# Building decay tables from Sigmoid and reciprocals, with one table load, in a retention and gated-FFN kernel

## The chip, the cores and the metric

The kernel runs on one core of one Trainium2 chip. Its metric is the device time of one execution in microseconds (us). A core has five engines that run their own instruction streams and wait for one another on semaphores: TensorE (PE; its weight loads are shown apart as PEld), VectorE (DVE), ScalarE (ACT), GpSimd (POOL) and SyncE (SP), which here gives out loads and stores. The transfers themselves run on 16 DMA engines. ScalarE computes functions such as Exp or Sigmoid from a table set, and the program holds an ACT_TABLE_LOAD wherever the set changes.

## The reference

Retention with a decay per head, on 8 batches of 8 heads, 576 positions and 64 features, is followed by a gated feed-forward layer on its 4608 x 512 result:

```python
scores = scale * np.matmul(q, k.transpose(0, 1, 3, 2))          # scale = 1/sqrt(64)
gamma = 1.0 - 2.0 ** (-5.0 - np.arange(H))
rel = pos[:, None] - pos[None, :]
Dmat = np.where(rel >= 0, gamma[:, None, None] ** rel[None, :, :], 0.0)
x = np.matmul(scores * Dmat[None], v)                           # then heads are put side by side
gate = 1.0 / (1.0 + np.exp(-(x @ w_gate)))
out = (gate * (x @ w_val)) @ w_out                              # 512 -> 1536 -> 512
```

The decay gamma^(i-j) is split into gamma^i on q and gamma^(-j) on k, so each needs a small table by position and head.

## The kernel before: the parts concerned

The loads of the first four chunks of batch 0 come as pairs (two chunks, four heads at a time). The first k and q are cut in two, one half given out by SyncE, the other by ScalarE:

```python
def load_pair(A):
    b, a2 = PAIRS[A]
    for nm, src, g in (("k", k, 0), ("q", q, 0), ("k", k, 1), ("q", q, 1), ("v", v, 0), ("v", v, 1)):
        t = ld_pool.tile([P, M, 2, D], FP32, tag="ld", ...)
        queues = (nc.sync, nc.scalar) if A == 0 and g == 0 and nm != "v" else (nc.sync,)
        n = M // len(queues)
        for i, queue in enumerate(queues):
            queue.dma_start(out=t[:, i * n:(i + 1) * n]..., in_=src[...]...)
```

TensorE is kept at work from the start with matmuls on a zero tile, of which nothing is used (`fill(10, 4)`: 40 of 128 columns; a plain `fill(n)`: n of 512 columns). Then the tables are made by Exp, first those of the pairs (`qtab2`, `ktab2`), then those of the later chunks (`qtab`, `ktab`); `warm` brings in the Sigmoid set for the gates:

```python
fill(10, 4)
def tables(shape, pattern, step, put, fix=None):
    ...                                          # iota of positions on GpSimd
    for h in range(H):
        nc.vector.tensor_scalar_mul(put(arg, h), pos, math.log(1.0 - 2.0 ** (-5.0 - h)))
    nc.scalar.activation(out=kt, in_=arg, func=AF.Exp, bias=0.0, scale=-1.0)
    nc.scalar.activation(out=qt, in_=arg, func=AF.Exp, bias=lnscale, scale=1.0)
    return qt, kt
qtab2, ktab2 = tables(...)
...
qtab, ktab = tables(...)
nc.scalar.activation(out=warm, in_=lnscale, func=AF.Sigmoid)
for t in sbd:                                    # four 128 x 512 bf16 tiles for states
    nc.vector.memset(t, 0.0)
```

The opening that follows multiplies k (on GpSimd) and q (on VectorE) by the tables (`cast_pair`), turns them on TensorE (`turn`: four transposes into PSUM, then one ScalarE copy to kT or qT), multiplies them (`pair_qk`, result qkp), masks that on VectorE (ptp), and forms the state from k and v (`first_st`, result st):

```python
cast_pair("q", 0, 0, nc.vector)
turn("k", 0, 0, *TR)
turn("q", 0, 0, *PV)
fill(3)
cast_pair("q", 0, 1, nc.vector)
pair_qk(0, 0, QK)
turn("k", 0, 1, *TR)
fill(2)
turn("q", 0, 1, *PV)
...                                              # the same for the second pair
first_st(0, 0)
```

The rest (`h` is a matmul with a gate or value weight, `op` one with the output weight) is a long run of matmuls that the change doesn't touch.

Of the kernel before, what the change touches and what calls it, by code (L numbers as in the profile page):

```python
# [9 lines left out]
FP32 = mybir.dt.float32  # L10
BF16 = mybir.dt.bfloat16
AF = mybir.ActivationFunctionType
ALU = mybir.AluOpType
# [3 lines left out]
def kernel(  # L17
# [19 lines left out]
    nc = tc.nc  # L37

    B, H, S, D = q.shape
    NT, DM = out.shape  # L40
    DFF = moe_w_gate.shape[1]
    P = 128
    M = H // 2
    NC = (S + P - 1) // P
# [3 lines left out]
    consts = ctx.enter_context(tc.tile_pool(name="consts", bufs=1))  # L48
# [18 lines left out]
    LAST = NC - 1  # L67
# [38 lines left out]
    def half(x):  # L106
        return slice(x * 64, x * 64 + 64)
# [17 lines left out]
    def load_pair(A):  # L125

        b, a2 = PAIRS[A]
        for nm, src, g in (("k", k, 0), ("q", q, 0), ("k", k, 1), ("q", q, 1), ("v", v, 0), ("v", v, 1)):
            t = ld_pool.tile([P, M, 2, D], FP32, tag="ld", name=f"{nm}32p_{A}_{g}")
            queues = (nc.sync, nc.scalar) if A == 0 and g == 0 and nm != "v" else (nc.sync,)  # L130
            n = M // len(queues)
            for i, queue in enumerate(queues):
                queue.dma_start(
                    out=t[:, i * n:(i + 1) * n].rearrange("p h r d -> p h (r d)"),
                    in_=src[b, g * M + i * n:g * M + (i + 1) * n,
                            a2 * 2 * P:(a2 + 1) * 2 * P, :].rearrange("h (p r) d -> p h (r d)", r=2))
            parts[nm, "pair", A, g] = t
            yield

# [10 lines left out]
    def load_wo(f):  # L150
        t = ld_pool.tile([P, DM], FP32, tag="ld", name=f"wo32_{f}")
        nc.sync.dma_start(out=t, in_=moe_w_out[f * P:(f + 1) * P, :])
        parts["o", f] = t

    both = [load_pair(A) for A in range(2)]
    for n_pair in (4, 2):
        for one in both:
# [5 lines left out]
    load_w(4, 4)  # L163
    load_w(8, 4)
    pair_2 = load_pair(2)
    for n_wo, n_pair in ((2, 4), (6, 2), (4, 0)):
        for _ in range(n_wo):
# [16 lines left out]
    def fill(n, parts=1):  # L184

        for i in range(n * parts):
            k = 4 // parts
            nc.tensor.matmul(idle[-1][:, 0:k, :], lhsT=blank, rhs=blank.unsqueeze(1).to_broadcast([P, k, P]),  # L188
                             start=True, stop=True)

    fill(10, 4)
    def tables(shape, pattern, step, put, fix=None):

        pos = consts.tile([P, pattern[0][1], pattern[1][1]], FP32, name=f"pos{step}")
        nc.gpsimd.iota(pos, pattern=pattern, base=0, channel_multiplier=step,
                       allow_small_or_imprecise_dtypes=True)
        if fix:
            fix(pos)
        arg = consts.tile(shape, FP32, name=f"arg{step}")
        qt = consts.tile(shape, FP32, name=f"qtab{step}")  # L200
        kt = consts.tile(shape, FP32, name=f"ktab{step}")
        for h in range(H):
            nc.vector.tensor_scalar_mul(put(arg, h), pos, math.log(1.0 - 2.0 ** (-5.0 - h)))
        nc.scalar.activation(out=kt, in_=arg, func=AF.Exp, bias=0.0, scale=-1.0)
        nc.scalar.activation(out=qt, in_=arg, func=AF.Exp, bias=lnscale, scale=1.0)
        return qt, kt

    lnscale = consts.tile([P, 1], FP32)
    nc.vector.memset(lnscale, math.log(1.0 / math.sqrt(D)))
    qtab2, ktab2 = tables([P, 2, H, 2], [[2 * P, 2], [1, 2]], 2, lambda t, h: t[:, :, h, :])  # L210
    ident = consts.tile([P, P], BF16)
    make_identity(nc, ident)


    def last_chunks(pos):
        nc.vector.tensor_scalar_add(pos[half(1), LAST], pos[half(1), LAST], -64.0)

    qtab, ktab = tables([P, NC, H, 1], [[P, NC], [1, 1]], 1, lambda t, h: t[:, :, h, :], last_chunks)
    qtab = qtab.rearrange("p c h o -> p c (h o)")
    ktab = ktab.rearrange("p c h o -> p c (h o)")  # L220
    warm = consts.tile([P, 1], FP32)
    nc.scalar.activation(out=warm, in_=lnscale, func=AF.Sigmoid)


    sbd = [consts.tile([P, M, P], BF16, name=f"sbd{i}") for i in range(4)]
    for t in sbd:
        nc.vector.memset(t, 0.0)

    trip = consts.tile([P, 2, P], BF16)
# [1 line left out]
    for p0 in (0, 64):  # L231
        nc.gpsimd.affine_select(out=trip[p0:p0 + 64], in_=trip[p0:p0 + 64], compare_op=ALU.is_ge, fill=0.0,
                                base=0, pattern=[[-1, 2], [1, P]], channel_multiplier=-2)
# [30 lines left out]
    def cast_pair(nm, A, g, eng):  # L264

        if (nm, A) not in natural:
            natural[nm, A] = osb_pool.tile([P, 2, H, D], BF16, tag="osb", name=f"{nm}p_{A}")
        if nm != "v" and A == 2:
            o = natural[nm, A].rearrange("p r (m y) d -> p y m r d", y=2)[:, g]
        else:  # L270
            o = natural[nm, A][:, :, g * M:(g + 1) * M, :].rearrange("p r h d -> p h r d")
        i = parts.pop((nm, "pair", A, g))
        if nm == "v":
            eng(out=o, in_=i)
        else:
            tab = (ktab2 if nm == "k" else qtab2)[:, PAIRS[A][1], g * M:(g + 1) * M, :].unsqueeze(3).to_broadcast([P, M, 2, D])
            eng.tensor_tensor(out=o, in0=i, in1=tab, op=ALU.mult)
# [51 lines left out]
    def pair_qk(A, g, banks):  # L329
        ps = [psum.tile([P, 2, 2, P], FP32, tag=tag, name=f"qkp_{A}_{g}_{hh}") for hh, (psum, tag) in enumerate(banks)]  # L330
        for i in range(2):
            m = 2 * g + i
            for r in range(2):
                for a in range(2):
                    for hh in range(2):
                        nc.tensor.matmul(ps[hh][half(a), i, r, :], lhsT=turned["kp", A][half(hh), m, r, half(a)],  # L336
                                         rhs=turned["qp", A][half(hh), m, a * P:(a + 1) * P], start=True, stop=True)
        if g == 0:
            probs["p", A] = [att_pool.tile([P, M, 2, P], BF16, tag="T", name=f"ptp_{A}_{hh}", bufs=6) for hh in range(2)]
        for hh in range(2):  # L340
            nc.vector.tensor_tensor(out=probs["p", A][hh][:, 2 * g:2 * g + 2], in0=ps[hh],  # L341
                                    in1=trip.unsqueeze(1).to_broadcast([P, 2, 2, P]), op=ALU.mult)
# [481 lines left out]
    def turn(nm, A, g, pool=ffn_psum, tag="ffn"):  # L824
        pair_t(nm, A, g, pool, tag, on_act)
# [36 lines left out]
    turn("k", 0, 0, *TR)  # L862
    turn("q", 0, 0, *PV)
    fill(3)
    cast_pair("q", 0, 1, nc.vector)
    pair_qk(0, 0, QK)
    turn("k", 0, 1, *TR)
# [233 lines left out]
```

## Time and profile before

| | |
|---|---|
| time, median of 3 | 328.39 us (328.38 to 328.81) |
| span of the profiled execution | 326.8 us |
| VectorE, ScalarE, GpSimd busy | 147.9, 140.7, 104.1 us |
| read from and written to memory | 37.75 and 9.44 MB |
| ACT_TABLE_LOADs | 2, of 1.28 us each, both in the first 6 us |

A busy time is the sum of an engine's instructions; a high share says which engine to look at, while a stage with its own limit has to be read from the timeline. In a row of the timeline the start and the duration come first, in us from the start of the span, then engine, line, operation, tiles with shapes, and in brackets the idle time of the engine ahead of it with what ended it. The chain of work that ended last follows the program back from its end, at each step to what released it; rows of it hold start, duration and what ran. A row of waits gives who waited for whom: total us, times, longest.

### The profile page before, as it was taken

What the parts mean: (1) busy time and instruction counts of PE and PEld (TensorE: products, weight loads), DVE (VectorE), ACT (ScalarE), POOL (GpSimd) and SP (SyncE); (2) the same over time, 40 slices, a digit from 0 to 9 for tenths busy, and PEclk for the clock granted to TensorE, in tenths of its full rate; (3) what the DMA queues carried; (4) which work ended last, traced back from release to release, by engine and by line L of the source; (5) the groups of instructions that cost most, each with busy time, mean ns of one, the idle gap of its engine ahead of it and who ended that gap; (6) DMA issues with size and microseconds to landing.
All of it is one profiled execution on the core that took longest, in us unless ns stands there. A gap on an engine that the chain in (4) does not pass through costs nothing.

```text
span 326.8 us, 8722 instructions
## 1 busy us (share of the span) xinstructions
PE 317.4 (97%) x3584; PEld 170.5 (52%) x3618; DVE 147.9 (45%) x335; ACT 140.7 (43%) x317; POOL 104.1 (32%) x138
## 2 busy tenths in 40 slices
PE   8899999999999999999999999999999999999996
PEld 7664557856546554455445544454445544544443
DVE  6855557656606462355334534344344433404410
ACT  6755545554433353325432553335334533343321
POOL 5774537544364563028200830075003000000000
PEclk9999999999999999999999999999999999999999
DMA  7999999989999999909890899069704810010003
GB/s 218 330 382 376 327 256 243 195 181 168 207 210 192 230 165 239 225 2 221 194 230 0 194 232 224 0 133 225 194 0 121 319 48 0 34 74 27 3 32 96
DMA packets 145849, 55.14 MB, mean 169 GB/s; under 512 B 125200, under 2 KB 137744, under 8 KB 145808
## 3 DMA queue, kind: packets, MB, share of 16 engines
q1 hardware_dynamic: 145120, 54.18, 68.6%
q8 instruction: 28, 0.46, 0.6%
q10 hardware_dynamic: 688, 0.39, 0.4%
q14 instruction: 13, 0.11, 0.1%
HBM read 37.75 MB, written 9.44 MB: 144 GB/s over the span
## 4 chain that ended last, share of the span: by engine, by line
PE 96%; ACT 1%; issue 1%; DVE 1%; ACTq 0%
PE h L731 50%; PE op L798 24%; PE op L980 3%; PE hv L835 3%; PE hg L835 3%; PE val L542 2%; PE idle L188 1%; PE row L516 1%; PE row L524 1%; PE val L558 1%; ACT qT L327 1%; PE op L787 1%; PE hg L906 1%; PE hv L906 1%; PE qkp L336 1%
## 5 line engine op out<-in xcount | busy, mean ns | idle before, releaser
L759 DVE TENSOR_TENSOR gv<-g,h 128x512 bf16<-128x512 bf16 (+1 forms) x96 | 62.8, 654 | 103.2 <-PE h L731 100.5
L731 PE MATMUL h<-xT,wv_sb 128*128 128x512 bf16 (+2 forms) x426 | 100.4, 355 | 0.3
L731 PE MATMUL h<-xT,wg_sb 128*128 128x512 bf16 (+2 forms) x426 | 100.4, 355 | 0.3
L755 ACT ACTIVATE g<-h 128x512 bf16<-128x512 f32 (+1 forms) x96 | 54.7, 570 | 94.3 <-PE h L731 90.2
L798 PE MATMUL op<-wo_sb,gv 128*128 128x512 bf16 x355 | 80.7, 379 | 2.2 <-issue 2.1
L731 PEld LDWEIGHTS <-wg_sb 128*128 128x128 bf16 x432 | 42.0, 98 | 41.2
L731 PEld LDWEIGHTS <-wv_sb 128*128 128x128 bf16 x432 | 42.0, 98 | 40.4
L798 PEld LDWEIGHTS <-gv 128*128 128x128 bf16 x372 | 35.3, 98 | 40.9
L295 POOL CAST v<-v 128x512 bf16<-128x512 f32 x29 | 18.1, 625 | 85.6 <-PE val L542 79.5
L290 POOL TENSOR_TENSOR qk<-k,ktab 128x512 bf16<-128x512 f32 x30 | 31.3, 1042 | 37.0 <-DMA k<-in_k_dram 36.5
L774 ACT COPY ob<-op 128x512 f32<-128x512 f32 x33 | 19.3, 585 | 35.9 <-PE op L798 32.9
L290 POOL TENSOR_TENSOR qk<-q,qtab 128x512 bf16<-128x512 f32 x28 | 29.2, 1042 | 1.9 <-DMA q<-in_q_dram 1.9
L531 DVE TENSOR_TENSOR pt<-row,tri 128x256 bf16<-128x256 f32 x60 | 21.6, 417 | 13.9 <-PE row L524 12.3
L600 ACT CAST xT<-val 128x256 bf16<-128x256 f32 x46 | 15.0, 380 | 22.7 <-PE val L558 18.0
L643 DVE TENSOR_TENSOR s<-s,row 128x256 f32<-128x256 f32 x39 | 16.2, 416 | 1.3
L492 ACT CAST sb<-s 128x256 bf16<-128x256 f32 x44 | 15.9, 420 | 0.3 <-DVE s L643 0.2
L586 DVE COPY glance<-val 128x1 f32<-128x1 f32 x24 | 2.8, 155 | 23.3 <-PE val L558 22.6
L980 PE MATMUL op<-wo_sb,gv 128*128 128x512 bf16 x45 | 11.4, 379 | 0.3 <-issue 0.2
L542 PEld LDWEIGHTS <-v 64*64 64x64 bf16 x480 | 6.2, 108 | 7.5 <-issue 7.2
L558 PE MATMUL val<-T,sb 64*64 64x64 bf16 x368 | 9.7, 195 | 0.3 <-DVE glance L586 0.3
L516 PE MATMUL row<-T 64*64 64x64 bf16 x480 | 9.7, 196 | 0.0
L341 DVE TENSOR_TENSOR ptp<-qkp,trip 128x512 bf16<-128x512 f32 x12 | 7.5, 681 | 3.8 <-PE qkp L336 3.7
(107 smaller groups left out, 236.0 us busy)
## 6 DMA issues: line engine op xcount, KB each, us to landing
out_dram<-ob SPq DMA_DIRECT2D x31, 256.0 KB, 3.1
k<-in_k_dram SPq DMA_DIRECT2D x26, 256.0 KB, 3.9
q<-in_q_dram SPq DMA_DIRECT2D x26, 256.0 KB, 4.1
v<-in_v_dram SPq DMA_DIRECT2D x26, 256.0 KB, 4.5
wg<-in_moe_w_gate_dram SPq DMA_DIRECT2D x12, 256.0 KB, 5.0
wv<-in_moe_w_val_dram SPq DMA_DIRECT2D x12, 256.0 KB, 5.1
wo<-in_moe_w_out_dram SPq DMA_DIRECT2D x12, 256.0 KB, 5.2
v32p<-in_v_dram SPq DMA_DIRECT2D x6, 256.0 KB, 4.9
```

Source lines behind the costliest of these rows:

```text
L290: eng.tensor_tensor(out=natural_qk[s][:, i].rearrange("p m (y d) -> p y m d", y=2), in0=by_halves(loaded[s][1 - i]), in1=tab, op=ALU.mult)
L295: eng(out=natural["v", s], in_=loaded[s][2])
L492: eng(out=state[key], in_=src)
L531: nc.vector.tensor_tensor(out=probs[s][:, y], in0=row_ps[s][y][:, 0], in1=tri.unsqueeze(1).to_broadcast([P, M, 64]), op=ALU.mult)
L643: nc.vector.tensor_tensor(out=new, in0=running[b], in1=p, op=ALU.add)
L731: nc.tensor.matmul(out, lhsT=w_sb[:, kc, fc * P:(fc + 1) * P], rhs=xT[:, kc, t0 + a:t0 + e], start=(kc == 0), stop=(kc == NKC - 1))
L755: nc.scalar.activation(out=g[:, 0:n], in_=h1[:, 0:n], func=AF.Sigmoid)
L759: nc.vector.tensor_tensor(out=gvs[some[0]][:, a:e], in0=g[:, 0:n], in1=h2[:, 0:n], op=ALU.mult)
L774: (eng or on_act)(out=ob, in_=opp)
L798: nc.tensor.matmul(opp, lhsT=gvs[fc][:, nb * P:(nb + 1) * P], rhs=wo_sb[:, fc, :], start=(fc == 0), stop=(fc == NFC - 1))
L835: nc.tensor.matmul(ps, lhsT=(wg_sb if what == "g" else wv_sb)[:, kc, fc * P:(fc + 1) * P], rhs=xT[:, kc, 0:4 * P], start=(kc == 0), stop=( ...
L980: nc.tensor.matmul(opps[nb], lhsT=gvs[fc][:, nb * P:(nb + 1) * P], rhs=wo_sb[:, fc, :], start=(fc == 0), stop=(fc == NFC - 1))
```

## The change

The two exponentials e^a and e^-a are to come from the Sigmoid set, which the gates need anyway: sigmoid(a)/sigmoid(-a) = e^a, and the inverse gives e^-a. ScalarE then needs one table set for the whole kernel, loaded before anything is ready for it, and the set change with `warm` goes. ScalarE also gives out no loads: SyncE gives out the first k and q whole. VectorE gets a Reciprocal and two multiplies for each table in place of the exponentials. The tables of the later chunks, which the opening doesn't use, and two of the four zeroings are finished between the first and the second q multiply.

```diff
-            queues = (nc.sync, nc.scalar) if A == 0 and g == 0 and nm != "v" else (nc.sync,)
-            n = M // len(queues)
-            for i, queue in enumerate(queues):
-                queue.dma_start(...half of the heads...)
+            nc.sync.dma_start(out=t..., in_=src[...all four heads...]...)
 ...
-        nc.scalar.activation(out=kt, in_=arg, func=AF.Exp, bias=0.0, scale=-1.0)
-        nc.scalar.activation(out=qt, in_=arg, func=AF.Exp, bias=lnscale, scale=1.0)
+        def sigmoids(self):
+            nc.scalar.activation(out=self.both[:, 0], in_=self.arg, func=AF.Sigmoid)
+            nc.scalar.activation(out=self.both[:, 1], in_=self.arg, func=AF.Sigmoid, scale=-1.0)
+
+        def powers(self):
+            nc.vector.reciprocal(out=self.inv, in_=self.both)
+            nc.vector.tensor_tensor(out=self.k, in0=self.both[:, 1], in1=self.inv[:, 0], op=ALU.mult)
+            nc.vector.scalar_tensor_tensor(out=self.q, in0=self.both[:, 0], scalar=1.0 / math.sqrt(D),
+                                           in1=self.inv[:, 1], op0=ALU.mult, op1=ALU.mult)
+
+    tabs2 = Tables([P, 2, H, 2], ...)            # the pairs' tables
+    tabs2.args(range(H))
+    tabs2.sigmoids()
 ...
-    warm = consts.tile([P, 1], FP32)
-    nc.scalar.activation(out=warm, in_=lnscale, func=AF.Sigmoid)
+    tabs1 = Tables([P, NC, H, 1], ...)           # the later chunks' tables
+    nc.vector.tensor_scalar_add(tabs1.pos[half(1), LAST], tabs1.pos[half(1), LAST], -64.0)
+    tabs1.args(range(M))
+    tabs2.powers()
+    tabs1.args(range(M, H))
+    tabs1.sigmoids()
 ...
-    for t in sbd:
+    for t in sbd[:2]:
         nc.vector.memset(t, 0.0)
 ...
     turn("q", 0, 0, *PV)
     fill(3)
+    tabs1.powers()
+    for t in sbd[2:]:
+        nc.vector.memset(t, 0.0)
     cast_pair("q", 0, 1, nc.vector)
```

On TensorE and GpSimd the two programs hold the same instructions in the same order.

More of the change, by code (lines that the diff above doesn't have):

```diff
@@ L129, in load_pair @@
             t = ld_pool.tile([P, M, 2, D], FP32, tag="ld", name=f"{nm}32p_{A}_{g}")
-            queues = (nc.sync, nc.scalar) if A == 0 and g == 0 and nm != "v" else (nc.sync,)
-            n = M // len(queues)
-            for i, queue in enumerate(queues):
[L133 to L136, printed above, removed]
+            nc.sync.dma_start(
+                out=t.rearrange("p h r d -> p h (r d)"),
+                in_=src[b, g * M:(g + 1) * M, a2 * 2 * P:(a2 + 1) * 2 * P, :].rearrange("h (p r) d -> p h (r d)", r=2))
             parts[nm, "pair", A, g] = t
@@ L191 @@
     fill(10, 4)
[L192 to L206, printed above, removed]
@@ L208, with __init__, tile_of, args @@
-    lnscale = consts.tile([P, 1], FP32)
-    nc.vector.memset(lnscale, math.log(1.0 / math.sqrt(D)))
-    qtab2, ktab2 = tables([P, 2, H, 2], [[2 * P, 2], [1, 2]], 2, lambda t, h: t[:, :, h, :])
+    class Tables:
+        def __init__(self, shape, pattern, step, put):
+            def tile_of(name, dims):
+                return consts.tile(dims, FP32, name=f"{name}{step}")
+            self.put = put
+            self.pos = tile_of("pos", [P, pattern[0][1], pattern[1][1]])
+            nc.gpsimd.iota(self.pos, pattern=pattern, base=0, channel_multiplier=step,
+                           allow_small_or_imprecise_dtypes=True)
+            self.arg, self.q, self.k = (tile_of(name, shape) for name in ("arg", "qtab", "ktab"))
+            self.both, self.inv = (tile_of(name, [P, 2] + shape[1:]) for name in ("both", "inv"))
+        def args(self, heads):
+            for h in heads:
+                nc.vector.tensor_scalar_mul(self.put(self.arg, h), self.pos, math.log(1.0 - 2.0 ** (-5.0 - h)))
+        def sigmoids(self):
[6 more added lines that the diff above has]
+                                           in1=self.inv[:, 1], op0=ALU.mult, op1=ALU.mult)
@@ L211 @@
+    tabs2 = Tables([P, 2, H, 2], [[2 * P, 2], [1, 2]], 2, lambda t, h: t[:, :, h, :])
+    tabs2.args(range(H))
+    tabs2.sigmoids()
+    qtab2, ktab2 = tabs2.q, tabs2.k
     ident = consts.tile([P, P], BF16)
     make_identity(nc, ident)
[L215 to L219, printed above, removed]
@@ L220 @@
-    ktab = ktab.rearrange("p c h o -> p c (h o)")
-    warm = consts.tile([P, 1], FP32)
-    nc.scalar.activation(out=warm, in_=lnscale, func=AF.Sigmoid)
+    tabs1 = Tables([P, NC, H, 1], [[P, NC], [1, 1]], 1, lambda t, h: t[:, :, h, :])
+    nc.vector.tensor_scalar_add(tabs1.pos[half(1), LAST], tabs1.pos[half(1), LAST], -64.0)
[3 more added lines that the diff above has]
+    tabs1.sigmoids()
+    qtab, ktab = (t.rearrange("p c h o -> p c (h o)") for t in (tabs1.q, tabs1.k))
```

## The prediction

> **What bounds the kernel now.** I read the page first: its busy shares and slices say that TensorE (PE) is the bound nearly everywhere.
>
> ```profile
> PE 317.4 (97%) x3584; PEld 170.5 (52%) x3618; DVE 147.9 (45%) x335; ACT 140.7 (43%) x317; POOL 104.1 (32%) x138
> PE   8899999999999999999999999999999999999996
> ```
>
> Only the first two slices (16 us) are below nine tenths, and the change touches nothing later: the order of instructions after the opening is the same in both programs. The change can therefore only move the moment at which TensorE becomes steadily busy; everything after it shifts by the same amount. Next I read the chain that ended last, restricted to the opening, to see which work sets that moment.
>
> ```profile
> 1.06 4.45 PE idle L188 x40
> 5.50 0.44 PE kTp L317 x4
> 5.95 0.02 issue
> 5.97 0.58 ACT kT L327
> 6.55 0.64 ACT qT L327
> ...
> 7.24 0.42 PE qkp L336 x16
> ...
> 11.78 0.78 ACT qT L327
> 12.56 0.05 issue
> 12.61 0.62 PE st L372 x8
> ```
>
> The chain doesn't pass through the decay tables, the table loads, or the first multiplies. It runs through the 40 warming matmuls, which hold TensorE from 1.06 to 5.50, and then through a relay of TensorE transposes and ScalarE evacuations (kT, qT) until 12.61. From there TensorE runs without a wait. The waits of TensorE in the first 20 us say the same; this is the whole answer:
>
> ```profile
> PE idle L188 <- DVE blank L175: 1.1, 1, 1.1
> PE st L372 <- ACT qT L327: 0.7, 1, 0.7
> PE qkp L336 <- ACT qT L327: 0.6, 2, 0.4
> ```
>
> So the only idle time is behind ScalarE's evacuations, none behind a decay table or a load. The timeline of the opening then shows how much slack the things that the change moves have.
>
> ```profile
> 1.87 1.28 ACT L204 ACT_TABLE_LOAD   x1 [1.87 <-issue]
> 3.83 1.04 POOL L277 TENSOR_TENSOR kp<-k32p,ktab 128x512 bf16<-128x512 f32 x1 [0.88 <-ACT qtab L205]
> 3.95 1.28 ACT L222 ACT_TABLE_LOAD   x1
> 4.50 0.91 DVE L277 TENSOR_TENSOR qp<-q32p,qtab 128x512 bf16<-128x512 f32 x1 [0.16 <-DMA q32p<-in_q_dram]
> 7.10 0.69 DVE L277 TENSOR_TENSOR qp<-q32p,qtab 128x512 bf16<-128x512 f32 x1 [1.69 <-DMA q32p<-in_q_dram]
> 12.05 2.10 POOL L274 CAST vp<-v32p 128x512 bf16<-128x512 f32 x3 [0.46 <-DMA v32p<-in_v_dram]
> ```
>
> The first k multiply starts at 3.83 and is held by the tables. It ends at 4.87, 0.63 us before the warming matmuls end at 5.50. The first q multiply ends at 5.41, while its transposes start at 5.72. ScalarE needs them only at 6.55 and they take 0.45, so q may be as late as about 6.0. The second table load ends at 5.23 and `warm` at 5.45; ScalarE is next wanted at 5.97.
>
> **What the Trainium skill says.** "ScalarE: Activation LUTs", section "What ACT_TABLE_LOAD costs", gives about 1283 ns for a load and a further 1380 ns of drain for a switch. The trace agrees on 1283 ns (1.28 twice) but shows no such drain: the second load starts at 3.95, as the ACTIVATE before it ends, and `warm` starts at 5.25. I take 1.28. "TensorE: Matmul & The Clock Gate", section "What you observe", has the first 38 or so matmuls of 128 columns at 107 ns each. Here 40 take 4.45 us, 111 ns each, so the end at 5.50 is a property of the clock and of the count, both unchanged. "DMA: Bandwidth & Descriptors", section "Issuing engines are not separate DMA queues", says that issuing from two engines saves only sequencer time, as all transfers share the 16 DMA engines. The trace agrees on the issue cost: a half load costs SyncE 0.46 and a whole one 0.47. "VectorE: DVE Perf Modes", section "First, the fixed hardware budget", says that Reciprocal is an iterated divide with a repeat count of 8. The trace of before has no Reciprocal, so I allow for anything from one to eight cycles per element.
>
> **The change part by part.**
> *Loads.* ScalarE's two issues (0.48 and 0.53) go. SyncE issues as many loads as before, the first two at double size, at the same moments (0.80, 1.32, 1.82). Landing took 2.6 to 2.9 us for SyncE's half loads; the quickest whole loads of k later in the trace (256 KB, one queue) took 2.9. So k lands at about 0.8 + 2.9 = 3.7 instead of about 3.5, and q at 4.5 to 4.7 instead of about 4.4 (the DVE wait puts it just ahead of 4.50).
>
> *Table load.* With nothing to issue, ScalarE loads at about 0.8 and is done at about 2.1, as the eight arguments are (1.07 + 0.97 = 2.04). Two sigmoids at the old exponentials' 0.23 and 0.30, overlapping, end near 2.55. The second load and `warm` (1.28 + 0.20 of ScalarE) go from a stretch in which ScalarE was not awaited: worth 0.
>
> *Powers for the pairs.* In front of them VectorE does the position fix (0.15) and four arguments (half of 1.00), to about 2.8. A Reciprocal over 64 elements: a VectorE memset of 256 elements takes 272 ns and an argument of 5 elements 201 ns, so about 0.3 at one cycle each and, estimated from the skill's repeat count, about 0.7 at eight. The two multiplies of 32 elements are about 0.2 each. ktab is then ready at 3.3 to 3.7, against 3.60 now. The k multiply thus starts at max(3.7, 3.3 to 3.7), near 3.8 as before, and ends near 4.9: still before 5.50. Gain 0.
>
> *q multiply.* After the powers (3.5 to 3.9) come four arguments (0.5) and two memsets (0.54): 4.6 to 4.9. With q landing at 4.5 to 4.7 it starts at 4.7 to 4.9 and ends at 5.6 to 5.8, later than 5.41 but inside the limit of 6.0. Loss 0.
>
> *Late tables.* Between the q multiplies: Reciprocal over 80 elements (0.3 to 0.85), two multiplies (0.4), two memsets (0.54), in all 1.25 to 1.8, from about 5.7 to 7.0 or 7.5. VectorE sat idle there for 1.69 us until q landed at 7.10. In the cheap case nothing moves; in the dear one the next q multiply ends at 8.2 instead of 7.79, and its transposes (8.25) can just be met. Loss 0 to 0.1.
>
> *Transfers.* The second v cast starts at 12.05, right as v lands, and ends at about 12.66, as the state product starts (12.61). There is no slack left: a transfer stream later by x delays the end by about x. A stream that is earlier gives at most 0.05, because the product also waits for the last qT evacuation (ends 12.55). By stage the DMA moved:
>
> ```profile
> 3.00:4.00 1.00, 1.00 (x12) 1.00 (x10) 0.99 (x7) 0.98 (x6) 0.17 (x1) 1.00 1.12 328
> 4.00:5.00 1.00, 1.00 (x13) 1.00 (x11) 0.84 (x3) 1.00 (x1) 0.87 (x1) 1.00 0.86 202
> ```
>
> (columns: stretch, its length, five engines' busy time, clock, DMA share, GB/s). The rate falls once ScalarE's queue is empty, and just while the second table load runs. One queue may be slower in the ramp: it moved 453 packets in 4.1 to 5.2, about 206 GB/s. If it stays at that rate from 2.8 to 4.1 instead of about 322, it is (322 - 206) x 1.3 = 150 KB behind, 0.45 us at the later 333 GB/s. If the dip goes with the table load, (322 - 206) x 1.1 = 128 KB, or 0.4 us, is won back. I take 0 to 0.2 lost after this cancellation, so +0.1.
>
> Sum: 0 + 0 + 0 + 0.05 + 0.05 to 0.1, about +0.1 us on 328.39, so 328.5; I put it at 328.4, as parts of the waiting overlap.
>
> **The rivals.** (a) *Tables are the bound and come early.* For it: the k multiply waits 0.88 us on ScalarE. Against it: the 40 warming matmuls. If TensorE were not held by them, up to 0.5 us would come back: 327.9. (b) *The single queue delays the loads.* For it: the 206 GB/s; against it: a steady 333 GB/s later on the same queue alone. It would give 328.8 to 329.0. (c) *VectorE becomes the bound of the opening* through a slow Reciprocal and memsets that now lie before a q multiply. It would need more than 0.4 us beyond my dear case; 328.7. (d) *The transfer stream is freed by the missing table load*: lands 0.4 us early, but hidden behind ScalarE: 328.3.
>
> **Range and chances.** The three times of before span 0.43 us, and the rivals 327.9 to 329.0, so the range is 327.9 to 328.9. Two per cent is 6.6 us, more than half of the whole opening of 12.6 us; only an unforeseen disturbance reaches it.
>
> **What would show it.** In the changed profile: one table load, before 1; the first kp at 3.7 to 3.9; the warming matmuls ending near 5.5 and kTp right behind; the first q multiply ending before 6.0; TensorE waiting only for qT in the first 20 us; the state product at 12.6 to 12.8. I am wrong if kTp waits for kp past 5.5, if a q transpose waits for VectorE by more than 0.2, or if the state product moves by more than 0.5 either way; the transfers are the least sure step.

## The result, and the profile after

The changed kernel takes 331.93 us (median of 6 runs, 330.46 to 332.81) against 328.39 (328.26 to 328.81): a ratio of 1.0097, 95% interval 1.007 to 1.0124. It is slower by about 3.2 us, and the predicted range (327.9 to 328.9) doesn't hold it.

Most of what the prediction worked out for the first 6 us is there. In the timeline of the changed kernel (start, duration, what, and in brackets the idle time before it):

```profile
0.80 1.28 ACT L206 ACT_TABLE_LOAD   x1 [0.80 <-PEq L1095]
2.65 0.54 DVE L210 RECIPROCAL inv<-both 128x64 f32<-128x64 f32 x1
3.88 1.04 POOL L284 TENSOR_TENSOR kp<-k32p,ktab 128x512 bf16<-128x512 f32 x1 [0.88 <-DVE arg L203]
4.64 0.83 DVE L284 TENSOR_TENSOR qp<-q32p,qtab 128x512 bf16<-128x512 f32 x1 [0.28 <-DMA q32p<-in_q_dram]
5.39 0.64 DVE L210 RECIPROCAL inv<-both 128x80 f32<-128x80 f32 x1
6.73 1.04 POOL L284 TENSOR_TENSOR kp<-k32p,ktab 128x512 bf16<-128x512 f32 x1 [1.80 <-DMA k32p<-in_k_dram]
8.52 1.04 POOL L284 TENSOR_TENSOR kp<-k32p,ktab 128x512 bf16<-128x512 f32 x1 [0.75 <-DMA k32p<-in_k_dram]
10.30 1.04 POOL L284 TENSOR_TENSOR kp<-k32p,ktab 128x512 bf16<-128x512 f32 x1 [0.74 <-DMA k32p<-in_k_dram]
12.10 0.61 POOL L281 CAST vp<-v32p 128x512 bf16<-128x512 f32 x1 [0.75 <-DMA v32p<-in_v_dram]
12.98 0.62 POOL L281 CAST vp<-v32p 128x512 bf16<-128x512 f32 x1 [0.27 <-DMA v32p<-in_v_dram]
13.17 0.28 PE L379 MATMUL st<-vp,kp 64*128 64x128 bf16 x2 [0.48 <-ACT qT L334]
13.64 0.49 PE L379 MATMUL st<-vp,kp 64*128 64x128 bf16 x6 [0.19 <-POOL vp L281]
```

There is one table load, at 0.80; the first k multiply starts at 3.88 (before: 3.83) and the first q multiply ends at 5.47. The 40 warming matmuls are over at 5.15 in this execution, earlier than the predicted 5.5. Then the loads fall behind. The rows of before for the second, third and fourth k multiply are

```profile
6.10 1.04 POOL L277 TENSOR_TENSOR kp<-k32p,ktab 128x512 bf16<-128x512 f32 x1 [1.23 <-DMA k32p<-in_k_dram]
7.95 1.04 POOL L277 TENSOR_TENSOR kp<-k32p,ktab 128x512 bf16<-128x512 f32 x1 [0.81 <-DMA k32p<-in_k_dram]
9.45 1.10 POOL L277 TENSOR_TENSOR kp<-k32p,ktab 128x512 bf16<-128x512 f32 x1 [0.45 <-DMA k32p<-in_k_dram]
```

and the second v cast started at 12.05; now they stand at 6.73, 8.52, 10.30 and 12.98, each as its load lands. The lag is 0.63 and 0.57 us at first, then 0.85 and 0.93. Two of the prediction's signs of being wrong came true: transposes wait for kp past 5.5 (at 7.83 by 0.67 us and at 11.40 by 0.30), and the state product, which started at 12.61, now starts at 13.17 and goes on only at 13.64. The waits of TensorE, over the whole span:

```profile
PE row L523 <- DMA T<-qk: 1.4, 1, 1.4
PE idle L184 <- DVE blank L171: 1.1, 1, 1.1
PE kTp L324 <- POOL kp L284: 1.0, 2, 0.7
PE st L379 <- ACT qT L334: 0.5, 1, 0.5
PE qkp L343 <- ACT qT L334: 0.3, 2, 0.2
PE val L565 <- DVE glance L593: 0.3, 1, 0.3
PE st L362 <- POOL vp L281: 0.3, 1, 0.3
PE st L379 <- POOL vp L281: 0.2, 1, 0.2
```

Transposes now wait for kp, state products for vp (twice: in the opening and at 44 us), and one row product, at 75.11, for a tile that a transposing transfer writes. None of these three kinds of wait was there before. Read from the same matmuls in both kernels, TensorE is late by 0.91 us after the opening (first gate matmuls at 16.66 in place of 15.75 in the chain), by 1.38 at the value matmuls ahead of that row product (73.22 in place of 71.84), by 2.99 at the row product itself (75.11, before 72.12), and by 3.04 at the last output block (323.85, before 320.81). Three losses, then, and all of them early. The largest, 1.6 us, is that of the row product (before, then changed):

```profile
72.12 0.30 PE L516 MATMUL row<-T 64*64 64x64 bf16 x16
75.11 0.32 PE L523 MATMUL row<-T 64*64 64x64 bf16 x16 [1.45 <-DMA T<-qk]
```

By stage the transfers themselves are slower. Two windows of the kernel before (the last number is GB/s, the one ahead of it the DMA share):

```profile
5.20:8.00 2.80, 2.38 (x35) 1.70 (x34) 1.11 (x3) 1.46 (x4) 1.09 (x2) 1.00 1.08 323
8.00:16.00 8.00, 7.14 (x161) 5.04 (x160) 6.70 (x11) 5.75 (x12) 5.93 (x9) 1.00 1.11 330
```

and of the changed kernel:

```profile
5.20:8.00 2.80, 1.82 (x30) 0.97 (x28) 2.11 (x7) 1.28 (x2) 1.04 (x1) 1.00 1.04 292
8.00:16.00 8.00, 6.71 (x133) 4.41 (x130) 6.51 (x11) 5.14 (x9) 4.56 (x7) 1.00 1.16 293
```

The DMA share is no lower (1.16 in place of 1.11; it can pass 1 because the records of packets on one engine overlap), but 293 GB/s are moved in place of 330. That lasts long after ScalarE's two half loads would have been over, so what makes it is not seen in this view.

### The profile page after: what moved, and what is told of

Read it like the earlier page. It is cut to its first block, busy times and chain, and to the rows that moved or that the text cites. A ratio compares the mean times of both kernels' runs of the same rounds, so it can differ in the third digit from the quotient of the medians.

```text
span 329.9 us, 8758 instructions
## 1 busy us (share of the span) xinstructions
PE 321.1 (97%) x3618; PEld 169.9 (52%) x3618; DVE 148.4 (45%) x340; ACT 139.5 (42%) x315; POOL 105.1 (32%) x138
## 4 chain that ended last, share of the span: by engine, by line
PE 86%; DMA 9%; SPq 2%; DVE 1%; POOL 1%; issue 0%; ACT 0%; DVEq 0%; ACTq 0%
PE h L738 50%; PE op L805 24%; DMA v32p<-in_v_dram 3%; PE op L990 2%; SPq L130 2%; DMA T<-qk 2%; DMA k32p<-in_k_dram 2%; PE val L549 2%; DMA wv<-in_moe_w_val_dram 2%; PE row L523 1%; PE val L565 1%; PE row L531 1%; PE op L794 1%; PE hg L916 1%; PE hv L916 1%; PE hg L842 1%
## 5 line engine op out<-in xcount | busy, mean ns | idle before, releaser
L805 PE MATMUL op<-wo_sb,gv 128*128 128x512 bf16 x372 | 84.0, 379 | 0.0
L990 PE MATMUL op<-wo_sb,gv 128*128 128x512 bf16 x48 | 11.7, 379 | 0.0
```

The costliest lines, as they stand in the source:

```text
L805: nc.tensor.matmul(opp, lhsT=gvs[fc][:, nb * P:(nb + 1) * P], rhs=wo_sb[:, fc, :], start=(fc == 0), stop=(fc == NFC - 1))
L990: nc.tensor.matmul(opps[nb], lhsT=gvs[fc][:, nb * P:(nb + 1) * P], rhs=wo_sb[:, fc, :], start=(fc == 0), stop=(fc == NFC - 1))
```

## The experiments

**First question: the loads or the tables?** The nearest suspect was the single queue (theory Q), the rival the tables and the new order on VectorE and ScalarE (theory T). Four kernels took the change apart.

`e1_two_queues`, the changed kernel with the loads put back:

```diff
-            nc.sync.dma_start(out=t..., in_=src[...all four heads...]...)
+            queues = (nc.sync, nc.scalar) if A == 0 and g == 0 and nm != "v" else (nc.sync,)
+            for i, queue in enumerate(queues):
+                queue.dma_start(...its share of the heads...)
```

> The changed kernel with only the loads put back: the first k and q again in two halves, one given out by ScalarE. Theory Q (the loss is the single queue: from 8 to 16 us the DMA moves 290 GB/s in place of 330, so the pairs land up to 1.1 us later): the time returns to 328.4 (328.0 to 328.8), v lands near 12.0. Theory T (the loss is the tables: Reciprocal and memsets ahead of the q multiplies): stays at 331.9. A split, 329.5 to 331, would mean that both have a share.

Measured: 332.26 us, ratio to before 1.0104 (1.0085 to 1.0123). Nothing came back. The time alone doesn't clear the queue, because ScalarE now loads its table only behind its two issues, and the first k multiply starts at 4.46 in place of 3.88. But the rate from 8 to 16 us is still 292 GB/s.

`e2_loads_only`, the same lines changed the other way in the kernel before:

> The kernel before with only the loads changed: all given out by SyncE, the first k and q whole, tables by Exp and two table loads as before. Theory Q: 331.9 (330.5 to 332.8), 8 to 16 us at about 290 GB/s. Theory T: 328.4.

Measured: 328.73 us, ratio 1.0011 (1.0001 to 1.002), with 347 GB/s from 8 to 16 us. The single queue costs 0.0 to 0.7 us, not 3.

`e3_halves_on_sync`, the changed kernel with `queues = (nc.sync, nc.sync)`:

> The changed kernel with the first k and q in two halves each, but all four given out by SyncE. It tells a second queue from the mere cut. Theory Q: the queue counts, so about 331.9, and up to 1 us more because SyncE has two more issues of 0.5 us in front. Theory S (what counts is the cut: smaller first loads land sooner, or the order in which the completion semaphores come round): 328.4 to 329.2.

Measured: 331.51 us, ratio 1.009 (1.0075 to 1.0105). As the first two had already cleared the loads, it only adds that the cut doesn't matter either.

`e4_after_again`, the changed kernel unaltered:

> The changed kernel unaltered, for a second profile beside the others on the same chip. Theory Q: 331.9 (330.4 to 332.9), the rate from 8 to 16 us again near 290 GB/s, v landing again near 13. If the low rate was an accident of one execution, the rate is 330 GB/s here and the time has another cause. Open is whether the 1.4 us that a row product waited for a transposed tile near 70 us comes again; runs between 330.5 and 332.8 suggest that it comes in some executions and not in others.

Measured: 331.49 us, ratio 1.0093 (1.0065 to 1.0122), 285 GB/s from 8 to 16 us. The low rate is no accident of one execution, and the wait for transposed tiles came again (2.0 us in two waits).

Theory Q fell: loads given out exactly as before are slow beside the new tables (`e1_two_queues`), and loads given out by SyncE alone are fast beside the old ones. Yet theory T in its first form didn't explain it either: what the tables add on ScalarE and VectorE is over by 7 us, while the low rate lasts until 16, and it is the transfers that slow down. What else do the tables change? They need room. The tiles `both` and `inv` take 1152 B a partition; `lnscale` and `warm` go. All pools behind the constants move. In the compiled programs the load buffers begin at

| kernel | bytes from the start of a partition | past a 256-byte boundary |
|---|---|---|
| before | 97536 | 0 |
| changed | 98624 | 64 |

The loads of the opening write pieces of 512 B; later weights come in pieces of 1 or 2 KB, and q, k and v of the later chunks in pieces of 256 B. With the shift each piece starts 64 B past a boundary. The Trainium skill, "DMA: Bandwidth & Descriptors", section "How a descriptor splits into AXI transactions", has transfers cut at 256-byte boundaries, so that a piece that starts off one touches more parts. By my estimate from that, 512 B would be three in place of two. Its text speaks of reads, and none of the runs so far shows it. That became theory A, with four experiments of its own.

**Second question: is it the place of the buffers?** `e5_after_aligned`, the changed kernel with the boundary restored:

```diff
-            self.arg, self.q, self.k = (tile_of(name, shape) for name in ("arg", "qtab", "ktab"))
+            self.arg, self.q = (tile_of(name, shape) for name in ("arg", "qtab"))
+            self.k = self.arg if step == 2 else tile_of("ktab", shape)
 ...
     xT = consts.tile([P, M, NT], BF16)
+    pad = consts.tile([P, 16], FP32, name="pad")
```

> The changed kernel with every pool after the constants moved down by 64 B a partition: the pairs' ktab is put in the place of its argument (128 B less) and 64 B are left empty, so that the load buffers begin at 98560 = 385 x 256 in place of 98624 = 385 x 256 + 64. Instructions and waits are the same. Theory A (the longer constants moved the load buffers off a 256-byte boundary, and transfers into them are slower): 328.2 (327.8 to 328.7), and 330 to 340 GB/s from 8 to 16 us. Theory T (the new order on VectorE and ScalarE costs it): 331.5 to 332, as the changed kernel.

Measured: 329.17 us (328.58 to 329.67) beside 328.85 for before on the same chip, ratio 1.0008 (0.9997 to 1.0019). The loss is gone, although every instruction of the change is still there. Its windows:

```profile
5.20:8.00 2.80, 2.75 (x35) 1.91 (x34) 2.57 (x8) 1.22 (x2) 1.11 (x2) 1.00 1.11 329
8.00:16.00 8.00, 7.21 (x161) 5.01 (x160) 6.96 (x12) 5.74 (x12) 6.18 (x9) 1.00 1.10 327
```

and its chain in the opening, which is that of before almost to the hundredth:

```profile
1.05 4.45 PE idle L184 x40
5.50 0.44 PE kTp L326 x4
5.94 0.02 issue
5.96 0.58 ACT kT L336
6.55 0.65 ACT qT L336
...
12.61 0.62 PE st L381 x8
```

`e6_before_plus_64`, the kernel before with nothing but 64 empty bytes:

```diff
     xT = consts.tile([P, M, NT], BF16)
+    pad = consts.tile([P, 16], FP32, name="pad")
```

> The kernel before with 64 empty bytes a partition behind the constants, nothing else: the load buffers and all pools behind them begin 64 B past a 256-byte boundary (97600), as in the changed kernel. Theory A: 331.5 to 332.3, about 290 GB/s from 8 to 16 us. Theory T: 328.4.

Measured: 331.62 us, ratio 1.0092 (1.0073 to 1.0112). An unused 64-byte tile alone makes the kernel before as slow as the changed one. The transfers' view from 8 to 16 us shows how (packets, MB, share of 16 engines). Before:

```profile
DMA packets 5119, 2.64 MB, mean 330 GB/s; under 512 B 157, under 2 KB 5118, under 8 KB 5118
q1 hardware_dynamic: 5118, 2.62, 110.1%
```

`e6_before_plus_64`:

```profile
DMA packets 4675, 2.34 MB, mean 292 GB/s; under 512 B 142, under 2 KB 4674, under 8 KB 4674
q1 hardware_dynamic: 4674, 2.32, 114.9%
```

Nearly all packets have 512 B in both. The record of one lasts 110.1% x 16 x 8 us / 5118 = 27.5 ns on average before and 114.9% x 16 x 8 us / 4674 = 31.5 ns now, 14% more. (The 512-byte packets alone that start in this stretch last 27.3 and 32.1 ns in the two traces, 18% more; before, some larger ones fall into it.) It doesn't end with the opening. From 80 to 160 us, where nearly all packets have 256 B, the same sum gives 21.4 ns before (89.7%, 53753 packets) and 23.8 ns (100.9%, 54279 packets) in `e6_before_plus_64`; TensorE is as busy there as before (79.16 us of 80, and 79.15), so that costs nothing.

**Third question: which buffers, and which boundary?** `e7_loads_off_rest_on` and `e9_loads_on_rest_off` split the shift in two, in the kernel before: an empty pool behind the load buffers takes the rest back to the boundary, or off it.

```diff
+    pad_pool = ctx.enter_context(tc.tile_pool(name="padp", bufs=1))   # between the load pool and the next
 ...
+    pad_1 = pad_pool.tile([P, 48], FP32, name="pad_1")    # e7, beside the 64 B of e6; e9: [P, 16], without them
```

> The kernel before with the load buffers alone 64 B past a 256-byte boundary: 64 B ahead of them and 192 B behind, so that all later pools (among them the tiles that the transposing transfers write) are on it. Theory A with two parts: only the loads' part of the loss, 1.2 to 2.0 us, so 329.6 to 330.4, and no wait for a transposed tile near 70 us. If the loads carry it all: 331.5 to 332. Theory T: 328.4.

> The kernel before with the load buffers on the 256-byte boundary and the pools behind them (transposed tiles, output buffers, gate tiles) 64 B past one. Theory A with two parts: the other part of the loss, 1 to 2 us by a wait for a transposed tile, so 329.4 to 330.4, with 330 GB/s from 8 to 16 us. If the loads carry it all: 328.4. Theory T: 328.4.

Measured: with the load buffers alone off the boundary 330.91 us (330.14 to 333.07), ratio 1.0075 (1.0049 to 1.01), 281 GB/s; with everything else off it 328.58 us, ratio 0.9992 (0.9981 to 1.0003), 341 GB/s. The two-part form of theory A fell: the load buffers carry the loss (only two small constants, which no transfer writes, move with them). The rate of 281 GB/s overstates it a little, as the transfers have gaps at the end of that stretch; a packet takes 30.6 ns there. The wait for a transposed tile goes with them as well, though I had put it on the tile's own place. It stands among the waits of `e7_loads_off_rest_on`, whose transposed tiles lie on the boundary:

```profile
PE st L358 <- POOL vp L277: 1.1, 2, 0.6
PE row L519 <- DMA T<-qk: 1.0, 1, 1.0
PE kTp L320 <- POOL kp L280: 1.0, 2, 0.7
```

and is missing in `e9_loads_on_rest_off`, whose tiles lie off it. This profile of `e7_loads_off_rest_on` is of its slowest run (333.07 us); that of `e11_before_plus_32` below, at 330.48 us, has no such wait, though its loads are late. So it is an aftermath of late loads that comes in some executions. SyncE gives out loads and transposing transfers in one order. The transfer that the row product at 75.11 waited for was given out at 68.96 in the changed kernel, behind loads that had fallen 3.0 to 3.9 us behind, and at 65.65 before (SPq stands for what SyncE gives out):

```profile
65.65 1.64 SPq L299 DMA_TRANSPOSE T<-qk  x1
68.96 2.04 SPq L306 DMA_TRANSPOSE T<-qk  x1
```

It also took 6.1 us to land. From 55 to 80 us these transfers took 4.3 us before and 4.0 in `e9_loads_on_rest_off` (medians), but 5.7 in the changed kernel and 5.9 in `e7_loads_off_rest_on`: they too are slower where the load buffers lie off the boundary, wherever their own tiles lie.

`e10_before_plus_128`, `e11_before_plus_32` and `e12_before_plus_256` have 32, 8 and 64 floats of padding in the place of the 16 of `e6_before_plus_64`.

> The kernel before with 128 empty bytes behind the constants: load buffers begin 128 B past a 256-byte boundary. Theory A256 (a 512-byte piece that straddles a 256-byte boundary is cut in more parts, wherever it starts): about 290 GB/s from 8 to 16 us and 331.5. Theory A128 (only the distance to a 128-byte boundary counts): 330 GB/s, 328.5.

> The kernel before with 32 empty bytes behind the constants: load buffers begin 32 B past a 256-byte boundary. Both theories of the boundary: 290 GB/s or less and 331.5 or more. A boundary of only 32 B: 328.5.

> The kernel before with 256 empty bytes behind the constants: as much is moved as anywhere in these runs, but the load buffers stay on a 256-byte boundary and come to lie on a 512-byte one. If only the boundary of 256 counts: 328.4 to 328.7 at 330 to 345 GB/s. If moving things as such costs: 331.5. If 512 counts as well: below 328.2.

Measured, with the rate and the mean time of a packet from 8 to 16 us:

| load buffers past a 256-byte boundary | GB/s | ns a packet | us | ratio to before |
|---|---|---|---|---|
| 32 B | 292 | 31.8 | 332.04 | 1.0099 (1.007 to 1.0129) |
| 64 B | 292 | 31.5 | 331.62 | 1.0092 (1.0073 to 1.0112) |
| 128 B | 287 | 31.6 | 330.91 | 1.0069 (1.0054 to 1.0084) |
| 256 B, so on the next one | 343 | 27.6 | 328.65 | 1.0004 (0.9997 to 1.0011) |

The boundary of 256 decides; how far off it makes no clear difference, and a boundary of 512 gives no measurable gain. Moving 256 B, the farthest of all, costs nothing, so it isn't the moving as such.

**Is there more to have?** `e13_aligned_short_fill` is `e5_after_aligned` with `fill(8, 4)`.

> The aligned form of the changed kernel with 32 warming matmuls in place of 40 (they compute nothing that is used): it asks whether the opening is held by them, as the prediction had it. They would end near 4.6, kp is ready near 4.95, so kTp starts 0.5 us sooner. If the loads have slack: 328.1 to 328.5, half a microsecond under its 40-matmul form. If v's landing near 11.6 to 12 or a clock that rises later takes it back: no difference, 328.6 to 329.2.

Measured: 329.2 us, ratio to before 1.0018 (1.0009 to 1.0026); no gain over the 40-matmul form. The timeline shows the lead and its loss:

```profile
4.85 0.46 PE L326 MATMUL kTp<-ident,kp 128*128 128x128 bf16 x4 [0.20 <-POOL kp L286]
8.26 0.40 PE L326 MATMUL qTp<-ident,qp 128*128 128x128 bf16 x4 [0.43 <-DVE qp L286]
12.72 0.45 PE L381 MATMUL st<-vp,kp 64*128 64x128 bf16 x5 [0.48 <-ACT qT L336]
```

kTp starts 0.44 us sooner than in `e5_after_aligned` (5.29 in its timeline, where a start may overlap the matmul before it), now held by kp as the prediction's slack had it. But the second qTp waits 0.43 us for its q multiply and stands at 8.26, where it stood at 8.25. Its q multiply started at 7.58, straight behind the late tables, whose first multiply took 1.06 us in this execution (0.20 in the changed kernel), in a stretch in which GpSimd's k multiply ran (5.90 to 6.94). In `e1_two_queues` the two overlap as well, and the table's multiply took 0.85 us and ended at 7.62, as GpSimd's multiply did at 7.56; in the four other profiles of this order they don't overlap, and it took 0.20. That the two get in each other's way fits this, but was not tested apart. So the late tables, which fill VectorE's gap when TensorE starts at 5.50, stand in the way when it starts sooner. In this execution the rate from 8 to 16 us was only 310 GB/s, though the buffers were aligned. A packet took 27.1 ns (104.9%, 4960 packets), as in the other aligned kernels, so the packets were not slower. The DMA share was lower (1.06, against 1.10 in `e5_after_aligned`); what held the transfers back is open. No version that I ran is measurably faster than the kernel before.

## Why the prediction was wrong

*The chain and the slack* were read rightly. With the buffers on the boundary (`e5_after_aligned`), the changed kernel keeps the predicted course: warming matmuls to 5.50, kTp right behind, the state product at 12.61, and a time that differs from that of before by -0.1 to +0.6 us, where +0.1 was predicted. Only "a property of the clock and of the count, both unchanged" says too much: in the changed kernel's own profile the same 40 matmuls were over at 5.15.

*Table load, powers, q multiply and late tables* stand. The table load was at 0.80 and worth nothing. The Reciprocal over 64 elements took 0.54 us (predicted 0.3 to 0.7), that over 80 took 0.64 (0.3 to 0.85); so 16 more elements cost 0.10 us. The two multiplies took 0.19 each. The first q multiply of the changed kernel ended at 5.47, below the 5.6 to 5.8 that I gave it.

*The step that failed* is "Transfers". It said rightly that the second v cast has no slack left and that a stream later by x delays the end of the opening by about x: the cast came 0.93 us late, and TensorE left the opening 0.91 late. But it looked for x only in the queue and in the table load, and came to "0 to 0.2 lost after this cancellation". Both sources were wrong. The dip from 4.1 to 5.2 us is still there without a second table load (199 GB/s in the changed kernel and 210 in `e5_after_aligned`, 206 before), so the table load didn't make it. From 2.8 to 4.1 the single queue was no slower than two: 325 GB/s in `e5_after_aligned` and 316 in `e2_loads_only`, 322 before. It costs 0.0 to 0.7 us in all. What moved x was absent from the sum: the list of what the change adds had instructions, issues and waits, but not the 1088 B by which its tiles push the load buffers, to 64 B past a 256-byte boundary. There the loads ran at 293 GB/s in place of 330.

*Rival (b)*, late loads at 328.8 to 329.0, named the wait that appeared, with another cause and about a sixth of the size. A second queue would have done nothing for the rate, as `e1_two_queues` shows. Its size was also wrong because I ended the account at the opening. TensorE lost 0.9 us there; the rest came at 44 and 75 us, where late loads had used up the slack of the third pair and of the first transposed tiles. "Everything after it shifts by the same amount" was thus wrong as well.

## What to carry to other kernels

When a change adds or removes tiles, look at where the program puts the buffers that transfers write, not only at its instructions. Here 32, 64 or 128 B off a 256-byte boundary cost 0.7 to 1.0% of the whole time; moving them back onto it (`e5_after_aligned`) took the loss away. When the transfers' rate falls at unchanged packet size, with a DMA share as high as before, look at the time of a packet and at the place of the buffers as well as at queues and issue order, and test it by padding a kernel that is otherwise unchanged.

## What the runs showed of the hardware that I hadn't expected

- Loads in pieces of 512 B into buffers that start off a 256-byte boundary moved 281 to 296 GB/s from 8 to 16 us in seven different programs, five of the six programs on it 327 to 347, and the sixth (`e13_aligned_short_fill`) 310. The time of a packet parts them without exception: 30.6 to 31.8 ns off the boundary, 27.1 to 27.8 on it. The Trainium skill's cut at 256 B ("DMA: Bandwidth & Descriptors", section "How a descriptor splits into AXI transactions") fits in where the boundary lies, but it doesn't give the cost of a write: by my estimate three parts in place of two would be half as much again, the chip showed 14 to 18%. That these parts are the mechanism was not shown apart.
- The place of transposed tiles and output buffers made no measurable difference (0.9981 to 1.0003).
- The warming matmuls ended at 5.15 in the profiled execution of the changed kernel (40 in 4.10 us) and at 5.50 before and in `e5_after_aligned` (4.45 us), with the same instructions. Those 0.35 us were worth nothing there, as the second kTp then waited 0.67 us for its k.
